# Order of key and value transfers, and the place of the value products, in a cached-attention decode kernel

## The chip, the core and the metric

The kernel runs on one core of a Trainium2 chip. The metric is the device time of one execution in microseconds (us). Engine names follow the profile: PE is TensorE (PEld its weight loads), DVE is VectorE, ACT is ScalarE, POOL is GpSimd, and SP is SyncE, which here only issues DMAs.

## The reference, cut to what matters

One decode step of grouped-query attention over a cache, plus a token-mixing MLP on the same normalised input:

```python
q = (xn @ wq).reshape(B, 1, 32, 128)                  # B = 8 tokens, 32 query heads, 8 key/value heads
scores = einsum("bhqd,bhkd->bhqk", q, k) * 128**-0.5  # cache length 8192, head width 128
p = softmax(scores)
o = einsum("bhqk,bhkd->bhqd", p, v)
y = x + o.reshape(B, 1, 4096) @ wo + mixer(layernorm(xn), w1, b1, w2, b2)
```

All is float32. There are 8 x 8 = 64 pairs of a batch element and a key/value head. The keys of a pair are 8192 x 128 numbers (4096 KB), and so are its values. The query weights `wq` are 8192 KB, the output weights `wo` another 8192 KB.

## The kernel before, in words

**Buffers.** There are two key buffers `K[0]`, `K[1]` and two value buffers `V[0]`, `V[1]`, of 4096 KB each. `wq` is first read into the two value buffers, and `wo` at the end into the two key buffers (`WO`). A pair `s` uses the buffers of index `k = s % 2`. "K63" and "V63" below are the keys and values of pair 63.

**Slots.** The order of the instructions is written out by hand. The function `slot(s, k, ...)` (L365) is called once for each pair: slots 0 and 1 stand ahead of a loop, the loop body holds four slots with a stage boundary between them (L408 to L412), and slots 62 and 63 stand behind it. In a slot:

- DVE turns the keys of the pair in place, four transposes (`turn`, L238), with the transposed probabilities of the pair before between the first and the second (`sm_turn`, L267).
- PE multiplies the probabilities of pair s-1 with its values (`pv`, L274, 16 products), sums the row sums (`o_sums`, L295), adds the mixer's part (`mx_end`, L341), starts the mixer's next part (`mx_begin`, L325), and then makes the scores of pair s (`qk`, L244, 16 products).
- SP issues the values of pair s+1 (L379), which waits until `pv` has left that buffer, and then the keys of pair s+2 (L382), which waits until `qk` has left theirs. In slot 62 the first half of `wo` takes the keys' place, and in slot 63 the second half follows in four pieces (L384, L386).
- DVE picks the result of `pv` (`o_pick`, L279 to L282), PE places it (`o_place`, L285). ACT and POOL do the mixer (`mx_steps`, L329 to L337) beside this.
- Then comes the softmax: the row maximum on DVE (`sm_max`, L250), a small product on PE (L254) with two DVE steps (L255, L256) for the bias, the exponential on ACT (`sm_exp`, L259), the normalising of pair s-1 on DVE (`o_norm`, L298 to L300), and the product that places the probabilities (`sm_place`, L263). The next slot begins with the turning of the next keys.

**The loop's stages.** An engine goes into a slot of the loop only when all engines have finished the slot before the last one. Each engine signals this at a place of its own (`previous_stage_wait`). SP signals it when the transfers issued in that slot have landed.

**The ends.** `prologue_barrier` (L405) stands ahead of slot 0. Ahead of it the queries are projected (L207) and the first keys turned. V0 is issued ahead of the barrier (L358), V1 behind it. After slot 63 the kernel turns the last probabilities, gathers the results of the first seven batch elements (`regroup`, L418 to L423), makes `pv` of pair 63, picks its result (`o_last`, L288 to L291), and multiplies with `wo`: 24 large products (L436), two copies (L439, L440), four folding products (L442) and 32 small products (L445). A copy (L446) and the output DMA (L447) end it.

Of the kernel before, what the change touches and what calls it, by code (L numbers as in the profile page):

```python
# [14 lines left out]
B, D, HQ, HKV, SK, DH, F = 8, 512, 32, 8, 8192, 128, 1792  # L15
REP = HQ // HKV
P = 128
NT = SK // P
Q = 32
NB = P // Q  # L20
NG = NT // 16
NU = NT // NG
BS = Q // B
# [5 lines left out]
N_IT = B * HKV  # L29
NW = 24  # L30
# [4 lines left out]
def attn_mixer_kernel(ctx: ExitStack, tc: tile.TileContext, x, kc, vc, wq, wo, w1, b1, w2, b2, out):  # L35
    nc = tc.nc
# [12 lines left out]
    def misc():  # L49
        turns[0] += 1  # L50
        return MI[turns[0] % 2]
# [5 lines left out]
    V = [ring.tile([P, NT, DH], F32, name=f"v{k}") for k in range(2)]  # L57
# [8 lines left out]
    def load(to, src, n, pieces=(NT,)):  # L66
        rows = src.rearrange("b h (p t) d -> (b h) p t d", p=P)[n]
        at = 0
        for w in pieces:
            nc.sync.dma_start(to[:, at:at + w, :], rows[:, at:at + w, :])  # L70
            at += w
# [4 lines left out]
    def load_wo(a, pieces):  # L76
        rows = wo.rearrange("(p a c) n -> a p c n", p=P, a=2)[a]
        at = 0
        for w in pieces:
            nc.sync.dma_start(WO[a][:, at:at + w, :], rows[:, at:at + w, :])  # L80
            at += w
# [13 lines left out]
    quarter = [slice(j * D // NB, (j + 1) * D // NB) for j in range(NB)]  # L95
# [34 lines left out]
    fold = const.tile([P, Q], F32, name="fold")  # L130
# [19 lines left out]
    OX = const.tile([P, N_IT, REP, NB], F32, name="ox")  # L150
# [14 lines left out]
    xo = const.tile([P, 32, Q], F32, name="xo")  # L165
    nc.vector.memset(xo, 0.0)
    wide = const.tile([P, D], F32, name="wide")
# [4 lines left out]
    O = [ps_o.tile([P, 512], F32, name=f"o{k}") for k in range(2)]  # L172

    MH = ps_h.tile([P, 512], F32, name="mh")
    MI = [ps_m.tile([P, 512], F32, name=f"misc{k}") for k in range(3)]
# [26 lines left out]
    def q_project(between):  # L202
        hw = HKV // 2
        n = REP * DH
        for c in range(NC):
            for h in range(HKV):
                nc.tensor.matmul(S[h // hw][h % hw * Q:(h % hw + 1) * Q, :], xnT[:, c, :], WQ[c][:, h * n:(h + 1) * n],  # L207
                                 start=(c == 0), stop=(c == NC - 1))
        for a in range(2):
            q = t2k.tile([P, n], F32, name="t2k")  # L210
            nc.scalar.copy(q, S[a])
            mt = O[a]
            for r in range(REP):
                nc.tensor.transpose(mt[:, r * P:(r + 1) * P], q[:, r * DH:(r + 1) * DH], ident)
            qs = work.tile([P, hw, REP, B], F32, name="qs")
            nc.scalar.copy(qs, mt.rearrange("p (r h b) -> p h r b", r=REP, b=Q)[:, :, :, :B])
            between(a)
            mq = misc()
            w = hw * REP * B
            for j in range(NB):  # L220
                nc.tensor.matmul(mq[:, j * w:(j + 1) * w], rj[:, j].rearrange("p i d -> p (i d)"),
                                 qs.rearrange("p h r b -> p (h r b)"), start=True, stop=True)
            for h in range(hw):
                nc.vector.tensor_copy(QT[:, :, a * hw + h].rearrange("p b j r -> p j r b"),
                                      mq.rearrange("p (j h x) -> p h j x", j=NB, h=hw)[:, h].rearrange("p j (r b) -> p j r b", r=REP))
        WQ.clear()
# [9 lines left out]
    def turn(k, a, w=NT // 4):  # L236
        t = K[k][:, a:a + w, :].rearrange("p t d -> p (t d)")
        nc.vector.transpose(t, t)  # L238
# [22 lines left out]
    def sm_place(k):  # L261
        m = misc()
        nc.tensor.matmul(m, perm, PR[k], start=True, stop=True)  # L263
        return m
# [6 lines left out]
    def pv(k, u0=0, u1=NU):  # L271
        for u in range(u0, u1):
            c = u % NB
            nc.tensor.matmul(O[k][c * Q:(c + 1) * Q, :], PT[k][:, u * Q:(u + 1) * Q],  # L274
                             V[k][:, u * NG:(u + 1) * NG, :].rearrange("p t d -> p (t d)"),
                             start=(u < NB), stop=(u >= NU - NB))

    def o_pick(k):
        nc.vector.tensor_tensor(OM.rearrange("p (g d) -> p g d", g=NG), O[k].rearrange("p (g d) -> p g d", g=NG),  # L279
                                dm.unsqueeze(2).to_broadcast([P, NG, DH]), ALU.mult)  # L280
        nc.vector.tensor_add(OB, OM[:, :256], OM[:, 256:])
        nc.vector.tensor_add(OB[:, :DH], OB[:, :DH], OB[:, DH:])  # L282

    def o_place(k):
        nc.tensor.matmul(MH[:, k * REP:(k + 1) * REP], OB[:, :DH], sel, start=True, stop=True)  # L285

    def o_last(k):
        nc.vector.tensor_copy(OM[:, :256], O[k][:, :256])  # L288
        nc.scalar.copy(OM[:, 256:], O[k][:, 256:])
        for g in range(NG):  # L290
            nc.tensor.matmul(MH[:, k * REP:(k + 1) * REP], OM[:, g * DH:(g + 1) * DH], selg[:, g, :],  # L291
                             start=(g == 0), stop=(g == NG - 1))

    def o_sums(k):
        nc.tensor.matmul(MH[:, 64 + k * REP:64 + (k + 1) * REP], LR[:, k:k + 1].to_broadcast([P, P]), sel, start=True, stop=True)  # L295

    def o_norm(k, s):
        nc.vector.reciprocal(RD, MH[:, 64 + k * REP:64 + (k + 1) * REP])  # L298
        nc.vector.tensor_tensor(OS, MH[:, k * REP:(k + 1) * REP], RD, ALU.mult)  # L299
        nc.vector.tensor_tensor(OX[:, s], OS.unsqueeze(2).to_broadcast([P, REP, NB]),  # L300
                                block.unsqueeze(1).to_broadcast([P, REP, NB]), ALU.mult)

    proj, mixed = MH[:, P:2 * P], MH[:, 2 * P:3 * P]
# [35 lines left out]
    def mx_end(k):  # L339
        for j in range(NB):  # L340
            nc.tensor.matmul(mixed[j * Q:(j + 1) * Q, :], BW[k], ACC[:, quarter[j]], start=True, stop=True)  # L341
# [5 lines left out]
    m = misc()  # L347
# [7 lines left out]
            turn(0, k * quart)  # L355

    q_project(first_turns)
    load(V[0], vc, 0)  # L358
    q_place(0, 0)
    mx_table()  # L360
    mx_pick(0, 0)

    def slot(s, k, placed, left=2, loop=False):  # L365

        if placed is not None:
            turn(k, 0)
            sm_turn(1 - k, placed)
            for a in range(1, 4):  # L370
                turn(k, a * quart)
            pv(1 - k)
            o_sums(1 - k)
            mx_end(1 - k)
        mx_begin(k)
        if loop:
            tc.previous_stage_wait(nc.tensor.engine)
        if left:
            load(V[1 - k], vc, s + 1)  # L379
        qk(k)  # L380
        if left > 1:
            load(K[k], kc, s + 2)  # L382
        elif left:
            load_wo(0, (NT // REP,))  # L384
        else:
            load_wo(1, (NW - 16, 4, 3, 1))  # L386
        if placed is not None:
            o_pick(1 - k)
            o_place(1 - k)
        mx_steps(k, loop)  # L390
        if left:
            q_place(s + 1, 1 - k)
            mx_pick(1 - k, s + 1)
        if placed is not None:
            y_add()
        if loop:
            tc.previous_stage_wait(nc.vector.engine)
        sm_max(k)
        sm_bias()
        sm_exp(k)  # L400
        if placed is not None:
            o_norm(1 - k, s - 1)
        return sm_place(k)

    tc.prologue_barrier()  # L405
    m = slot(0, 0, None)
    m = slot(1, 1, m)
    with tc.For_i(2, N_IT - 2, 4, iteration_sync="staggered") as s:  # L408
        for n in range(4):
            m = slot(s + n, n % 2, m, loop=True)  # L410
            if n < 3:
                tc.stage_boundary()  # L412
    m = slot(N_IT - 2, 0, m, left=1)
    m = slot(N_IT - 1, 1, m, left=0)

    def regroup(b0, b1, copy):  # L418
        for b in range(b0, b1):
            nc.tensor.matmul(O[0][:, b * Q:(b + 1) * Q], OX[:, b * HKV:(b + 1) * HKV].rearrange("p h r j -> p (h r j)"), fold,  # L420
                             start=True, stop=True)
        copy(xo.rearrange("p c (b s) -> p c b s", s=BS)[:, :, b0:b1, 0],
             O[0][:, b0 * Q:b1 * Q].rearrange("p (b c) -> p c b", c=Q))  # L423

    sm_turn(1, m)
    regroup(0, B - 1, nc.scalar.copy)
    pv(1)
    o_sums(1)
    mx_end(1)
    o_last(1)  # L430
    o_norm(1, N_IT - 1)
    regroup(B - 1, B, nc.vector.tensor_copy)
    y_add()
# [4 lines left out]
        nc.tensor.matmul(proj[j * Q:(j + 1) * Q, :], gather[:, j].rearrange("p b s -> p (b s)"), yacc, start=True, stop=False)  # L438
    nc.vector.tensor_copy(wide[:, :256], S[0][:, :256])  # L439
    nc.scalar.copy(wide[:, 256:], S[0][:, 256:])  # L440
    for j in range(NB):
        nc.tensor.matmul(proj[j * Q:(j + 1) * Q, :], fold, wide[:, quarter[j]], start=False, stop=False)  # L442
    for c in range(NW, 32):
        for j in range(NB):
            nc.tensor.matmul(proj[j * Q:(j + 1) * Q, :], xo[:, c, :], WO[1][:, c - 16, quarter[j]], start=False, stop=(c == 31))  # L445
    nc.vector.tensor_copy(yacc, proj)  # L446
# [29 lines left out]
```

## Time and profile before

| what | value |
|---|---|
| median of 3 runs | 1298.3 us (1298.07 to 1300.26) |
| the profiled execution's own time | 1300.48 us |
| its span in the trace | 1298.7 us |
| bytes read from memory | 553.69 MB, 426 GB/s over the span |
| PE busy, mean granted clock | 905.7 us (70%), 0.77 |
| DVE, ACT, POOL busy | 857.5, 331.3, 218.0 us |

Times in the rows of the trace count from the start of the span. A row of the timeline has the start, the duration, the engine, the line, the operation, its operands with their sizes, and behind an "x" how many instructions it stands for; brackets tell how long the engine was idle before and for what. A row of the windows has the stretch, its length, the busy time of PE, PEld, DVE, ACT and POOL (each with a count), the granted PE clock, the busy share of the DMA engines and their GB/s. A matmul of float32 numbers shows as two records.

### The profile page before, as it was taken

The numbers are of one execution on the slowest core, as the hardware profiler recorded it, in microseconds if no ns is written. First come the engines' busy times: TensorE is split into PE (matmuls) and PEld (weight loads), VectorE is DVE, ScalarE is ACT, GpSimd is POOL, SyncE is SP. The second block draws the span as 40 slices with busy tenths as digits, with TensorE's granted clock in tenths as the row PEclk, the third lists the DMA queues.
The fourth block names the chain that finished last, engine by engine and source line by source line (L and its number), as shares of the span: only waits on it lengthen the run. The fifth ranks groups of instructions, "written<-read, shape, count | busy, mean of one in ns | idle before, by whom it ended". The sixth has DMA issues, their size and how long they took to land.

```text
span 1298.7 us, 15589 instructions
## 1 busy us (share of the span) xinstructions
PE 905.7 (70%) x5498; PEld 271.0 (21%) x5498; DVE 857.5 (66%) x1261; ACT 331.3 (26%) x458; POOL 218.0 (17%) x205
## 2 busy tenths in 40 slices
PE   4657767767767767766766766776766776776777
PEld 1112212212212212212212211221221221211223
DVE  3666766766766776776776776776676676676671
ACT  1223123223223223223223213213213312312321
POOL 1112122122112112112112112112112212212211
PEclk9678778778768778768777777867777877877877
DMA  9999999999999999999999999999999999999994
GB/s 405 435 433 426 432 435 436 436 432 428 432 436 436 435 432 428 433 436 436 434 432 428 434 436 436 434 432 428 434 436 436 433 429 432 434 436 436 433 427 196
DMA packets 19789, 553.84 MB, mean 426 GB/s; under 512 B 2332, under 2 KB 2364, under 8 KB 2628
## 3 DMA queue, kind: packets, MB, share of 16 engines
q1 hardware_dynamic: 19620, 553.67, 98.8%
q8 instruction: 7, 0.11, 0.0%
q0 software_dynamic: 160, 0.04, 0.0%
q14 instruction: 2, 0.02, 0.0%
HBM read 553.69 MB, written 0.02 MB: 426 GB/s over the span
## 4 chain that ended last, share of the span: by engine, by line
PE 58%; DVE 20%; issue 15%; DMA 6%; DVEq 1%; POOL 0%; ACT 0%; POOLq 0%
PE o L274 28%; PE s L244 17%; DVE k L238 8%; PE misc L325 5%; DMA k<-in_A_k_cache_dram 4%; DVE mr L250 3%; DVE pt L267 3%; DMA v<-in_A_v_cache_dram 3%; PE misc L254 2%; PE mh L341 2%; PE mh L285 2%; PE mh L295 2%; DVE sq L255 1%; DVE nb L256 1%; DVE os L299 1%
## 5 line engine op out<-in xcount | busy, mean ns | idle before, releaser
L238 DVE STREAM_TRANSPOSE k<-k 128x2048 f32<-128x2048 f32 x256 | 574.0, 2280 | 154.5 <-issue 131.2
L274 PE MATMUL o<-v,pt 128*32 128x512 f32 x2048 | 370.3, 889 | 193.3 <-DVE pt L267 191.8
L329 ACT ACT_TABLE_LOAD x64 | 82.1, 1283 | 799.0 <-PE misc L325 787.7
L244 PE MATMUL s<-k,w 128*32 128x512 f32 x2048 | 234.6, 599 | 0.0
L332 POOL TENSOR_TENSOR macc<-g,mw 112x512 f32<-112x512 f32 x64 | 66.7, 1042 | 989.4 <-ACT g L329 989.4
L274 PEld LDWEIGHTS o<-v,pt 128*32 128x32 f32 x2048 | 87.0, 155 | 504.4 <-issue 359.2
L263 PE MATMUL misc<-pr,perm 128*128 128x512 f32 x128 | 116.3, 1006 | 105.6 <-ACT pr L259 105.6
L306 DVE TENSOR_TENSOR yacc<-mh,yacc 128x128 f32<-128x128 f32 x64 | 18.7, 292 | 188.2 <-PE mh L285 188.2
L329 ACT ACTIVATE g<-misc,mw 112x512 f32<-112x512 f32 x128 | 99.5, 777 | 79.3 <-POOL macc L332 77.8
L244 PEld LDWEIGHTS s<-k,w 128*32 128x32 f32 x2048 | 60.2, 110 | 166.4 <-issue 140.9
L337 ACT ACT_TABLE_LOAD x64 | 82.1, 1283 | 1.1
L336 POOL TENSOR_TENSOR macc<-macc,g 112x512 f32<-112x512 f32 x64 | 80.8, 1263 | 5.1
L332 POOL TENSOR_TENSOR g<-g,mw 112x512 f32<-112x512 f32 x64 | 66.6, 1040 | 56.9 <-ACT g L329 56.9
L254 PE MATMUL misc<-nident,mr 128*128 128x128 f32 x128 | 31.2, 326 | 62.7 <-DVE mr L250 62.7
L325 PE MATMUL misc<-hn,bm 8*112 8x512 f32 x128 | 71.7, 640 | 0.6 <-DVE mw L315 0.6
L259 ACT ACTIVATE pr<-s,nb 128x512 f32<-128x512 f32 x64 | 44.0, 687 | 35.1 <-DVE rd L298 23.9
L263 PEld LDWEIGHTS misc<-pr,perm 128*128 128x128 f32 x128 | 25.8, 252 | 117.8 <-ACT pr L259 115.9
L250 DVE TENSOR_REDUCE mr<-s 128x1 f32<-128x512 f32 x64 | 43.6, 681 | 6.6 <-PE s L244 6.6
L267 DVE STREAM_TRANSPOSE pt<-misc 128x512 f32<-128x512 f32 x64 | 43.2, 675 | 2.5 <-PE misc L263 2.5
L279 DVE TENSOR_TENSOR om<-o,dm 128x512 f32<-128x512 f32 x63 | 41.7, 662 | 2.5 <-PE o L274 2.1
L255 DVE TENSOR_TENSOR sq<-misc,hmask 128x128 f32<-128x128 f32 x64 | 18.7, 292 | 37.1 <-PE misc L254 37.1
L254 PEld LDWEIGHTS misc<-nident,mr 128*128 128x128 f32 x128 | 19.0, 187 | 69.1 <-DVE mr L250 69.1
(98 smaller groups left out, 378.3 us busy)
## 6 DMA issues: line engine op xcount, KB each, us to landing
v<-in_A_v_cache_dram SPq DMA_DIRECT2D x64, 4096.0 KB, 19.8
k<-in_A_k_cache_dram SPq DMA_DIRECT2D x63, 4096.0 KB, 24.2
v<-in_A_wq_dram SPq DMA_DIRECT2D x2, 4096.0 KB, 17.0
k<-in_A_k_cache_dram SPq DMA_DIRECT2D x2, 2048.0 KB, 30.3
k<-in_A_wo_dram SPq DMA_DIRECT2D x1, 4096.0 KB, 25.2
k<-in_A_wo_dram SPq DMA_DIRECT2D x1, 2048.0 KB, 10.1
k<-in_A_wo_dram SPq DMA_DIRECT2D x1, 1024.0 KB, 12.2
k<-in_A_wo_dram SPq DMA_DIRECT2D x1, 768.0 KB, 13.5
```

Of the source, the lines that this page charges most:

```text
L238: nc.vector.transpose(t, t)
L244: nc.tensor.matmul(S[k][g * Q:(g + 1) * Q, :], W[k][:, j, :], kt[:, g, :, j * Q:(j + 1) * Q], start=(j == 0), stop=(j == NB - 1))
L250: nc.vector.tensor_reduce(MR, S[k], AX.X, ALU.max)
L254: nc.tensor.matmul(m[:, :P], MR.to_broadcast([P, P]), nident, start=True, stop=True)
L263: nc.tensor.matmul(m, perm, PR[k], start=True, stop=True)
L267: nc.vector.transpose(PT[k], m)
L274: nc.tensor.matmul(O[k][c * Q:(c + 1) * Q, :], PT[k][:, u * Q:(u + 1) * Q], V[k][:, u * NG:(u + 1) * NG, :].rearrange("p t d -> p (t d)"), ...
L325: nc.tensor.matmul(MI[2][:FP, :], BM[k].to_broadcast([B, FP]), hn, start=True, stop=True)
L329: nc.scalar.activation(G, MI[2][:FP, :], AF.Gelu_apprx_tanh, bias=MW[k][:, 1, j:j + 1], scale=MW[k][:, 0, j:j + 1])
L332: nc.gpsimd.tensor_tensor(G if j else ACC, G, MW[k][:, 2, j:j + 1].to_broadcast([FP, D]), ALU.mult)
L336: nc.gpsimd.tensor_add(ACC, ACC, G)
L337: nc.scalar.activation(sink, epst[:1], AF.Exp)
```

## The change

Five things change.

1. The values of pair s are issued as the first thing in slot s, no longer in slot s-1. So SP's order becomes: values of pair s, keys of pair s+2. The keys of a pair now stand ahead of the values of the pair before it. V0 is now issued behind the prologue's barrier. In slot 63 the first half of `wo` is issued right behind V63, the second half after `qk` as it was.
2. `pv` of pair s-1 leaves the start of slot s. Its first 8 products stand behind the softmax's bias, its last 8 behind the placing product. PE's stage signal stands between them.
3. `o_pick`, `o_place`, `o_sums` and `o_norm` in slot s are now those of pair s-2.
4. `regroup` of the first seven batch elements goes from behind slot 63 into it, ahead of `qk`, and uses another PSUM buffer.
5. At the end, `pv` of pair 63 stands in two halves around `o_pick` and `o_place` of pair 62, `o_last` stands ahead of `mx_end`, and the four folding products stand behind the first 16 of the 32 small products.

The core of the diff:

```diff
-    load(V[0], vc, 0)
     q_place(0, 0)
...
-    def slot(s, k, placed, left=2, loop=False):
+    def slot(s, k, placed, n, left=2, loop=False):
+        load(V[k], vc, s)
+        if not left:
+            load_wo(0, (NT // REP,))
+        if n:
             turn(k, 0)
             sm_turn(1 - k, placed)
             for a in range(1, 4):
                 turn(k, a * quart)
-            pv(1 - k)
-            o_sums(1 - k)
+        if n > 1:
+            o_sums(k)
+        if n:
             mx_end(1 - k)
         mx_begin(k)
-        if loop:
-            tc.previous_stage_wait(nc.tensor.engine)
-        if left:
-            load(V[1 - k], vc, s + 1)
+        if not left:
+            regroup(0, B - 1, nc.scalar.copy)
         qk(k)
         if left > 1:
             load(K[k], kc, s + 2)
-        elif left:
-            load_wo(0, (NT // REP,))
-        else:
+        elif not left:
             load_wo(1, (NW - 16, 4, 3, 1))
-        if placed is not None:
-            o_pick(1 - k)
-            o_place(1 - k)
+        if n > 1:
+            o_pick(k)
+            o_place(k)
...
         sm_exp(k)
-        if placed is not None:
-            o_norm(1 - k, s - 1)
-        return sm_place(k)
+        if n:
+            pv(1 - k, 0, NU // 2)
+        if loop:
+            tc.previous_stage_wait(nc.tensor.engine)
+        if n > 1:
+            o_norm(k, s - 2)
+        m = sm_place(k)
+        if n:
+            pv(1 - k, NU // 2, NU)
+        return m
...
     sm_turn(1, m)
-    regroup(0, B - 1, nc.scalar.copy)
-    pv(1)
+    pv(1, 0, NU // 2)
+    o_pick(0)
+    o_place(0)
+    o_sums(0)
+    o_norm(0, N_IT - 2)
+    pv(1, NU // 2, NU)
     o_sums(1)
+    o_last(1)
     mx_end(1)
-    o_last(1)
     o_norm(1, N_IT - 1)
...
-    for j in range(NB):
-        nc.tensor.matmul(proj[j * Q:(j + 1) * Q, :], fold, wide[:, quarter[j]], start=False, stop=False)
     for c in range(NW, 32):
+        if c == NW + 4:
+            for j in range(NB):
+                nc.tensor.matmul(proj[j * Q:(j + 1) * Q, :], fold, wide[:, quarter[j]], start=False, stop=False)
```

**SP, start of the program.** The rows show what SP issues before the loop, with the semaphores that it waits for. Here `k_81`, `k_82` are the two key buffers and `v_83`, `v_84` the two value buffers. Before:

```order
L70 DMA k_81<-in_A_k_cache_dram 128x4096 x2
L70 DMA k_82<-in_A_k_cache_dram 128x8192
L70 DMA v_83<-in_A_v_cache_dram 128x8192 [waits DMAHW0_49,PE_49]
L70 DMA v_84<-in_A_v_cache_dram 128x8192 [waits barrier_Pool_Activation_PE_DVE_SP_release,DMAHW1_49,PE_49]
L70 DMA k_81<-in_A_k_cache_dram 128x8192 [waits DMAHW2_49,DMAHW3_49,DVE_49,PE_49]
```

V0 (the first row of `v_83`) waited only for the transfer of `wq` and the PE products that read it. The same stretch of the changed kernel:

```order
L70 DMA k_81<-in_A_k_cache_dram 128x4096 x2
L70 DMA k_82<-in_A_k_cache_dram 128x8192
L70 DMA v_83<-in_A_v_cache_dram 128x8192 [waits barrier_Pool_Activation_PE_DVE_SP_release,DMAHW0_49,PE_49]
L70 DMA k_81<-in_A_k_cache_dram 128x8192 [waits DMAHW2_49,DMAHW3_49,DVE_49,PE_49]
L70 DMA v_84<-in_A_v_cache_dram 128x8192 [waits DMAHW1_49]
```

V0 now waits for the barrier, and K2 (the second row of `k_81`) stands ahead of V1.

**SP, end of the program.** The rows are the last transfers of the loop, the loop's end, and what follows. Before, the values of `v_83` are V62, the keys K63, and `v_84` behind the loop is V63:

```order
L70 DMA v_83<-in_A_v_cache_dram 128x8192
L70 ISA
L70 DMA k_82<-in_A_k_cache_dram 128x8192
L408 REGISTER_ALU
L408 COMPARE_AND_BRANCH
L408 UNCONDITIONAL_BRANCH
L70 DMA v_84<-in_A_v_cache_dram 128x8192
L80 DMA k_81<-in_A_wo_dram 128x8192
```

In the changed kernel K63 is the last transfer of the loop, ahead of V62 and V63:

```order
L70 DMA k_82<-in_A_k_cache_dram 128x8192
L421 REGISTER_ALU
L421 COMPARE_AND_BRANCH
L421 UNCONDITIONAL_BRANCH
L70 DMA v_83<-in_A_v_cache_dram 128x8192
L70 DMA v_84<-in_A_v_cache_dram 128x8192
L80 DMA k_81<-in_A_wo_dram 128x8192
```

K63 moved by one transfer of 4096 KB towards the start, and V62 by one towards the end. V63 and `wo` kept their places.

**PE, one slot of the loop.** Here `s_176` takes the scores, `o_178` and `o_177` the value products, `misc_180` and `misc_181` the small products of the softmax. Before:

```order
L274 MATMUL o_177<-v_83,pt_153 32x512 x16
L295 MATMUL mh<-sel,lr 128x4
L341 MATMUL mh<-macc,bw_171 32x128 x4
L325 MATMUL misc_182<-hn,bm_170 112x512
L244 MATMUL s_176<-k_82,w_152 32x512 x16
L285 MATMUL mh<-sel,ob 128x4
L254 MATMUL misc_180<-nident,mr 128x128
L263 MATMUL misc_181<-pr_156,perm 128x512
```

And in the changed kernel:

```order
L295 MATMUL mh<-sel,lr 128x4
L341 MATMUL mh<-macc,bw_171 32x128 x4
L325 MATMUL misc_182<-hn,bm_170 112x512
L244 MATMUL s_176<-k_82,w_152 32x512 x16
L285 MATMUL mh<-sel,ob 128x4
L254 MATMUL misc_180<-nident,mr 128x128
L274 MATMUL o_177<-v_83,pt_153 32x512 x8
L263 MATMUL misc_181<-pr_156,perm 128x512
L274 MATMUL o_177<-v_83,pt_153 32x512 x8
```

The value products moved from the time in which DVE turns the keys to both sides of the placing product.

More of the change, by code (lines that the diff above doesn't have):

```diff
@@ L393, in slot @@
             mx_pick(1 - k, s + 1)
-        if placed is not None:
+        if n:
             y_add()
@@ L400, in slot, with regroup @@
         sm_exp(k)
-        if placed is not None:
-            o_norm(1 - k, s - 1)
-        return sm_place(k)
+        if n:
[5 more added lines that the diff above has]
+        m = sm_place(k)
+        if n:
+            pv(1 - k, NU // 2, NU)
+        return m
+    def regroup(b0, b1, copy):
+        for b in range(b0, b1):
+            nc.tensor.matmul(MI[0][:, b * Q:(b + 1) * Q], OX[:, b * HKV:(b + 1) * HKV].rearrange("p h r j -> p (h r j)"), fold,
+                             start=True, stop=True)
+        copy(xo.rearrange("p c (b s) -> p c b s", s=BS)[:, :, b0:b1, 0],
+             MI[0][:, b0 * Q:b1 * Q].rearrange("p (b c) -> p c b", c=Q))
     tc.prologue_barrier()
-    m = slot(0, 0, None)
-    m = slot(1, 1, m)
+    m = slot(0, 0, None, 0)
+    m = slot(1, 1, m, 1)
     with tc.For_i(2, N_IT - 2, 4, iteration_sync="staggered") as s:
         for n in range(4):
-            m = slot(s + n, n % 2, m, loop=True)
+            m = slot(s + n, n % 2, m, 2, loop=True)
             if n < 3:
                 tc.stage_boundary()
[L413 to L423, printed above, removed]
-    sm_turn(1, m)
-    regroup(0, B - 1, nc.scalar.copy)
-    pv(1)
+    m = slot(N_IT - 2, 0, m, 2, left=1)
+    m = slot(N_IT - 1, 1, m, 2, left=0)
+    sm_turn(1, m)
+    pv(1, 0, NU // 2)
[4 more added lines that the diff above has]
+    pv(1, NU // 2, NU)
     o_sums(1)
+    o_last(1)
     mx_end(1)
-    o_last(1)
     o_norm(1, N_IT - 1)
```

## The prediction

> **What bounds the kernel now.** I read the page's slices and queues first, since a kernel that moves 554 MB may be bound by its transfers.
>
> ```profile
> DMA  9999999999999999999999999999999999999994
> GB/s 405 435 433 426 432 435 436 436 432 428 432 436 436 435 432 428 433 436 436 434 432 428 434 436 436 434 432 428 434 436 436 433 429 432 434 436 436 433 427 196
> q1 hardware_dynamic: 19620, 553.67, 98.8%
> ```
>
> The DMA engines are busy in every slice but the last. The windows place the end of that, and the rows of DVE give the pace of the loop: each slot starts when its keys land.
>
> ```profile
> 40.00:1270.00 1230.00, 868.91 (x5202) 254.56 (x5202) 834.47 (x1201) 325.72 (x446) 213.47 (x192) 0.76 1.00 433
> 1270.00:1281.00 11.00, 9.94 (x40) 4.92 (x44) 1.29 (x5) 1.35 (x3) 0.61 (x1) 0.55 0.94 400
> 1281.00:1283.30 2.30, 2.30 (x27) 1.15 (x19) 0.42 (x1) 0.37 (x1) 0.00 (x0) 0.93 0.24 95
> 1283.30:1298.70 15.40, 10.52 (x135) 4.72 (x135) 1.63 (x7) 0.37 (x1) 0.00 (x0) 0.88 0.01 2
> ...
> 72.53 2.31 DVE L238 STREAM_TRANSPOSE k<-k 128x2048 f32<-128x2048 f32 x1 [4.25 <-DMA k<-in_A_k_cache_dram]
> 1253.72 2.31 DVE L238 STREAM_TRANSPOSE k<-k 128x2048 f32<-128x2048 f32 x1 [2.94 <-DMA k<-in_A_k_cache_dram]
> ```
>
> From K2 (72.53) to K63 (1253.72) are 61 slots of 19.36 us. Two transfers of 4.194 MB at 433 GB/s are 19.37 us. So the loop runs at the pace of the DMA, which has no gap, and one transfer of 4096 KB takes 9.68 us. The transfers end near 1281.6 (0.24 x 2.3 us into the third window). The last 17 us of the span move nothing. The chain that ended last and SP's issues show what fills them.
>
> ```profile
> 1229.71 23.92 DMA k<-in_A_k_cache_dram
> ...
> 1275.96 6.24 PE o L274 x32
> 1282.20 0.32 PE mh L295 x2
> ...
> 1285.39 6.75 PE s L436 x48
> ...
> 1295.26 0.29 DVE yacc L446
> ```
>
> K63 lands at 1253.63, and turning, scores, softmax, the value product of pair 63, `wo` and the output follow one another. V63 and all of `wo` land meanwhile, so the last value product, which ends at 1282.20, is late by computation and not by data.
>
> **The change, part by part.** *Bytes.* The same transfers are made. If the DMA still has no gap, it ends where it did, plus what the start loses.
>
> *The start.* V0 now waits for the barrier. Its price is a possible gap behind K1.
>
> ```profile
> 0.75 0.86 SPq L63 DMA_DIRECT2D v<-in_A_wq_dram  x2
> 40.49 0.33 SPq L70 DMA_DIRECT2D v<-in_A_v_cache_dram  x1
> 47.73 0.33 SPq L70 DMA_DIRECT2D k<-in_A_k_cache_dram  x1
> 49.62 2.30 DVE L238 STREAM_TRANSPOSE k<-k 128x2048 f32<-128x2048 f32 x1
> ...
> 0.00:2.00 2.00, 0.00 (x0) 0.00 (x0) 0.00 (x0) 1.24 (x1) 0.93 (x6) 1.00 0.53 147
> 0.00:20.00 20.00, 6.37 (x36) 1.81 (x36) 7.89 (x33) 1.87 (x3) 3.92 (x13) 1.00 0.95 395
> 20.00:40.00 20.00, 7.63 (x64) 3.88 (x64) 11.75 (x16) 1.61 (x4) 0.00 (x0) 0.80 0.98 419
> ```
>
> By 40 us, 7.90 + 8.38 = 16.28 MB have moved. `wq`, K0 and K1 are 16.78 MB, so K1 runs until 41.15. V1 left right behind the barrier at 40.49, and V0 will now leave there. At the start of the run 0.29 MB had moved by 2.00, which is 0.68 us of full rate, so data flowed 0.6 us after the issue at 0.75. That would put V0's data at 41.1: no gap. The upper bound is the output transfer, issued at 1295.58 (row below), whose whole way takes until the span's end, 3.1 us: a gap of 2.4. I take 0.5 us, nearer to the first row. K2 is issued after the first scores (47.73) while V0 runs until 51, so nothing starves behind it.
>
> *The loop.* Rows of two slots give the pieces:
>
> ```profile
> 1225.93 3.64 PE L244 MATMUL s<-k,w 128*32 128x512 f32 x32
> 1230.87 0.49 PE L254 MATMUL misc<-nident,mr 128*128 128x128 f32 x2 [0.98 <-DVE mr L250]
> 1232.47 0.18 DVE L300 TENSOR_TENSOR ox<-os,block 128x16 f32 x1
> 1233.01 1.59 PE L263 MATMUL misc<-pr,perm 128*128 128x512 f32 x2 [1.66 <-ACT pr L259]
> 1234.47 2.31 DVE L238 STREAM_TRANSPOSE k<-k 128x2048 f32<-128x2048 f32 x1 [1.82 <-issue]
> 1237.30 6.66 DVE L238 STREAM_TRANSPOSE k<-k 128x2048 f32<-128x2048 f32 x3
> ...
> 1244.14 3.64 PE L244 MATMUL s<-k,w 128*32 128x512 f32 x32
> ```
>
> Scores start 9.7 us after the first turn (1244.14 - 1234.47), and DVE's last step of the softmax ends 3.1 us after the scores (1232.65 - 1229.57). So the next turn can start after 12.8 + q us, where q is the time of `qk`. Before, `qk` followed the value product directly and ran at full clock in 3.64 us. Now PE has little to do while DVE turns the keys, and `qk` comes behind a pause. What that costs is told by rows that come behind a pause:
>
> ```profile
> 42.43 5.24 PE L244 MATMUL s<-k,w 128*32 128x512 f32 x32
> 53.33 6.61 PE L274 MATMUL o<-v,pt 128*32 128x512 f32 x32 [1.57 <-DMA v<-in_A_v_cache_dram]
> 42.00:43.00 1.00, 1.00 (x5) 0.20 (x8) 0.00 (x0) 0.47 (x1) 0.00 (x0) 0.50 1.14 492
> 46.00:48.00 2.00, 1.66 (x16) 0.24 (x8) 0.18 (x1) 0.75 (x2) 1.64 (x2) 1.00 1.21 524
> L274 PE MATMUL o<-v,pt 128*32 128x512 f32 x2048 | 370.3, 889 | 193.3 <-DVE pt L267 191.8
> ```
>
> The first `qk` began at a clock of 0.50 and took 5.24; wholly at half clock it would be 7.3. I take 5.3, the row of the same product behind a pause, and a slot needs 18.1 us (16.4 to 20.1). The transfers give it 19.36, so the cover is 1.2 us and the edit costs nothing; beyond it every 0.1 us would cost 6 us over 62 slots. The Trainium skill, "TensorE: Matmul & The Clock Gate", section "Part 1: The HAM clock gate", says that PE runs at half rate after an idle window of about 3.4 us, and at full rate only after a busy window of that length. By that page `qk` would turn fast 3.4 to 6.8 us after its start, an estimate of 5.3 to 7.0 us for q and 18.1 to 19.8 for a slot; the trace agrees as to the half clock behind the pause.
>
> The softmax's own chain fits too: 1.3 us from scores to L254, 0.5 for it, half a value product (1.8 at full clock, as half of 3.64; 3.3 as half of 6.61), the placing product (1.6), then the other half. With q = 5.3 the value buffer is free 22 to 26 us after its slot's start. Values issued then have to start 38.7 us after it (four transfers later), and keys, issued after 15 us, 29.0 us after it. Each queue has over 12 us in hand. SP's signal, which waits for the transfers of the slot before the last, names keys that the slot needs anyway.
>
> *The end.* K63 now goes ahead of V62, so it lands at 1253.63 - 9.68 + 0.5 = 1244.4. V63 and `wo` keep their places:
>
> ```profile
> 1242.57 0.34 SPq L70 DMA_DIRECT2D v<-in_A_v_cache_dram  x1
> 1267.70 2.22 SPq L80 DMA_DIRECT2D k<-in_A_wo_dram  x4
> 1295.58 0.70 SPq L447 DMA_DIRECT2D out_dram<-yacc  x1
> ...
> L80 SPq DMA_DIRECT2D k<-in_A_wo_dram x5: 328/368/901, 1247.8 to 1269.0; - x5
> ...
> k<-in_A_wo_dram SPq DMA_DIRECT2D x1, 256.0 KB, 13.7
> ```
>
> The last piece of `wo` lands at 1269.0 + 13.7 = 1282.7, with the start's loss 1283.2. Behind it stand only the last small products and the copy; before, the copy began 3.44 us ahead of the span's end (1298.7 - 1295.26). With 0.3 us for the products this floor is 1283.2 + 0.3 + 3.4 = 1286.9 us.
>
> The engines may be later. From 1244.4: scores begin 9.7 us on and end at 1259.4 (q = 5.3), L254 ends 1.8 us on at 1261.2; then four halves of value products and the placing product in a row. At full clock these are 4 x 1.8 + 1.1 = 8.3 us, ending at 1269.5. At the mean of the group (370.3 / 64 = 5.8 for a whole product) they are 4 x 2.9 + 1.6 = 13.2 us, ending at 1274.4. From that end to the copy it was 13.1 us (1282.20 to 1295.26); the folding products behind half of the small ones hide some 0.4 of that in the wait for the copies, so 12.7. `regroup` in slot 63 lies under the turning and costs nothing; its 2.8 us also leave the chain of the end. At full clock the engines reach the copy at 1282.2, ahead of the floor; at the mean clock at 1287.1, and the span is 1290.5. PE has no pause behind `qk` here, so I lean to the faster case: 1288.6 us, 10.1 less than 1298.7.
>
> **The sum.** Span 1298.7 - 10.1 = 1288.6. The profiled execution's own time was 1300.48 and the median of the runs 1298.3; taking the 10.1 off the median gives 1288.2.
>
> **The rivals.** *A: the engines become the bound.* PE's pause makes `qk` slow in each slot, and the next turn waits for the softmax behind it. Slot 1 turns at 49.62, so slot 63 starts at 49.6 + 62c for a slot of c us. At c = 19.27 that is 1244.4, and nothing is lost; at 19.45 the whole gain is gone; at 19.7 it is 1271.0, 26.6 us late, and the time is 1315. For it: the half clock in rows above, and q = 6.9 is enough. Against it: `qk` itself is work that brings the clock back within 4 us (42.43 to 46). By that page of the Trainium skill c would be 18.9 in the mean, an estimate below the deciding 19.45. Chance of a loss beyond 0.2%: 0.08; of c near 19.45 and no change: 0.03.
>
> *B: the DMA gets gaps.* V63 waits for the second half of the value product of pair 61, 22 to 26 us into slot 62, and V62, ahead of it on the queue, is through 29.0 us into it. With a slow clock and slow issue it may be late by up to 2 us, and V0 by 2.4. Everything behind shifts: a span of 1290.5 to 1292.5, so 1290 to 1292. Against it stand the slacks worked out above. Chance 0.12, still faster.
>
> *C: the start of slot 63 is not the bound.* If the end is held by `wo` alone with no loss at the start, the floor is 1286.4, and the time 1286.0. Inside my forecast's range.
>
> **The chances.** The forecast (a loop at the DMA's pace, an end shortened by 8 to 12 us) has 0.77, B 0.12, A 0.11. The range goes from C (1286.0) to the end at the mean clock together with B's gap (1290.5 - 1298.7 + 1298.3 = 1290.1, plus 2.4) = 1292.5. About 0.2%, 2.6 us, is what a measurement of this kernel can tell: the three runs lie 2.2 us apart. Faster by more than that 0.89, within it 0.03, slower 0.08.
>
> **What would show it.** Right: the windows still show a share of 1.00 and 433 GB/s from 40 to 1270, slots of 19.36 us that start at the landing of keys, K63's first turn near 1244, and 6 to 8 us between the last transfer and the span's end. The row of `qk` should stand at 5 to 6 us in place of 3.64. Wrong: DVE's first turn waiting for its own softmax and not for keys (A), a gap in the DMA near 41 or near 1253 (B), or a last `wo` product that starts after 1281.

## The result and the profile after

The changed kernel takes 1289.8 us (median of 4 runs, 1289.41 to 1290.11), the kernel before 1298.35 us beside it (4 runs, 1298.07 to 1300.26). The ratio is 0.9931 (95% interval 0.9914 to 0.9948): 8.55 us less, where 10.1 were forecast. A later set of runs, nine of the kernel before and five of the changed one beside them, gave 1300.24 and 1289.6 us: 10.6 us less. The experiment "Before, again" says why the kernel before gives two such medians. The profiled execution of the changed kernel took 1290.11 us, its span is 1288.2 us.

First the slices' GB/s and the queue on the page after:

```profile
GB/s 408 418 428 437 427 435 439 426 438 432 431 439 426 436 434 430 438 427 435 436 428 438 431 432 439 425 438 433 430 439 427 435 436 428 438 429 433 439 426 348
q1 hardware_dynamic: 19620, 553.67, 99.7%
```

The last slice moves 348 GB/s where it moved 196, and the queue's share rose from 98.8% to 99.7%. The bytes are the same, so the time saved is time in which nothing was moved. The windows after (us from the span's start, length, then busy time of PE, PEld, DVE, ACT and POOL, the granted clock, the DMA's share and GB/s) say where:

```profile
42.00:43.00 1.00, 1.00 (x5) 0.20 (x8) 0.00 (x0) 0.31 (x2) 0.00 (x0) 0.50 0.13 33
40.00:1260.00 1220.00, 830.92 (x5176) 241.76 (x5176) 871.20 (x1191) 326.31 (x447) 216.12 (x192) 0.80 1.00 433
1260.00:1272.00 12.00, 10.70 (x84) 3.48 (x76) 4.96 (x15) 0.80 (x3) 0.00 (x0) 1.00 0.98 421
1282.00:1283.30 1.30, 1.16 (x40) 0.89 (x35) 0.00 (x0) 0.25 (x1) 0.00 (x0) 1.00 0.43 167
```

The loop keeps a share of 1.00 at 433 GB/s. The microsecond from 42 to 43 moves 33 GB/s, where before it moved 492: that is the gap of the start, 0.9 us. Counted at the full rate, the transfers then end near 1282.5 (0.43 x 1.3 us into the fourth window), 5.7 us before the span's end; before, counted the same way, they ended near 1281.6, 17.1 us ahead of it. That is 11.4 us less behind the data and 0.9 us more ahead of its end: 10.5 us of span, 1298.7 to 1288.2.

The chain that ended last, after (start, duration, what), then the record of SP's last four issues of `wo` (shortest, median and longest, first and last start) and the time from issue to landing of the last two:

```profile
1221.04 23.93 DMA k<-in_A_k_cache_dram
...
1245.06 2.31 DVE k L238
...
1261.66 21.98 DMA k<-in_A_wo_dram
...
1283.68 1.12 PE mh L456 x32
...
1284.82 0.29 DVE yacc L457
...
L80 SPq DMA_DIRECT2D k<-in_A_wo_dram x4: 328/427/432, 1260.8 to 1262.1; - x4
k<-in_A_wo_dram SPq DMA_DIRECT2D x1, 768.0 KB, 22.0
k<-in_A_wo_dram SPq DMA_DIRECT2D x1, 256.0 KB, 22.1
```

K63 is turned at 1245.06 and no longer at 1253.72. The chain before ran from K63 to the copy over the engines, 48 records of `wo` products (6.75 us) among them; now it runs through a transfer of `wo`, with 16 small products (32 records) and the copy behind it. With its 21.98 us that transfer is the piece of 768 KB, the last but one, which lands at 1283.64. The last piece, of 256 KB, lands near 1284.2 (1262.1 + 22.1). Only the last 4 of the 16 products need it; 12 of 16 take some 0.8 of the 1.1 us, so PE comes to them near 1284.5 and does not wait. PE's rows of the end say how near the engines are to that floor:

```profile
1279.42 1.92 PE L446 MATMUL s<-k,xo 128*32 128x512 f32 x16 [0.94 <-DMA k<-in_A_wo_dram]
...
1283.68 1.08 PE L456 MATMUL mh<-k,xo 128*32 128x128 f32 x32 [0.52 <-DMA k<-in_A_wo_dram]
```

PE waits for `wo` at the last large products for 0.94 us: the engines are ahead of the data, but by no more than that.

The loop pays elsewhere for what it got. These are the scores and the value products, first in the page before, then in the page after (busy us and mean ns of one):

```profile
L244 PE MATMUL s<-k,w 128*32 128x512 f32 x2048 | 234.6, 599 | 0.0
```

```profile
L244 PE MATMUL s<-k,w 128*32 128x512 f32 x2048 | 372.6, 894 | 324.6 <-DVE k L238 324.6
L274 PE MATMUL o<-v,pt 128*32 128x512 f32 x2048 | 246.0, 598 | 0.0
```

The half clock behind PE's pause has moved from the value products (370.3 before, 246.0 after) to the scores: 372.6 / 64 = 5.82 us for a pair. The waits of DVE ahead of its turns (us in all, times, longest), and its first turn in slot 1, give what is left of the cover:

```profile
DVE k L238 <- issue: 45.7, 50, 1.7
...
50.81 2.30 DVE L238 STREAM_TRANSPOSE k<-k 128x2048 f32<-128x2048 f32 x1
```

From 50.81 to 1245.06 are 62 slots of 19.26 us. DVE waits ahead of its first turn for 45.7 us in all, 0.74 us a slot; before, the same wait was 131.2 us. The 19.26 and the 0.74 are means over two stretches. From 89.64 to 276.97 are ten slots of 18.73 us in the mean, in which DVE waits only twice (1.2 us in all): the keys are there, and the engines set the pace. That shows the engines' slot directly, 18.6 us without the two waits. The rows at both ends of that stretch:

```profile
89.64 2.31 DVE L238 STREAM_TRANSPOSE k<-k 128x2048 f32<-128x2048 f32 x1
...
276.97 2.31 DVE L238 STREAM_TRANSPOSE k<-k 128x2048 f32<-128x2048 f32 x1
```

From 276.97 to 1245.06 the slots are 19.36 us, the transfers' pace of before, and DVE waits 0.88 us a slot. There the transfers set the slot, with little to spare.

### The profile page after: what moved, and what is told of

Its sections match the earlier page's. It is cut to its first block, busy times and chain, and to the rows that moved or that the text cites. A ratio compares the mean times of both kernels' runs of the same rounds, so it can differ in the third digit from the quotient of the medians.

```text
span 1288.2 us, 15580 instructions
## 1 busy us (share of the span) xinstructions
PE 866.7 (67%) x5498; PEld 256.0 (20%) x5498; DVE 897.4 (70%) x1261; ACT 331.3 (26%) x458; POOL 220.0 (17%) x205
## 3 DMA queue, kind: packets, MB, share of 16 engines
q1 hardware_dynamic: 19620, 553.67, 99.7%
## 4 chain that ended last, share of the span: by engine, by line
DVE 49%; PE 35%; issue 9%; DMA 6%; DVEq 0%; SPq 0%; ACT 0%; ACTq 0%
DVE k L238 39%; PE s L244 28%; DMA k<-in_A_k_cache_dram 4%; DVE pt L267 3%; DVE mr L250 2%; PE misc L254 2%; DMA k<-in_A_wo_dram 2%; PE mh L285 2%; DVE sq L255 1%; PE o L274 1%; DVE nb L256 1%; DVE os L299 1%; PE misc L263 1%; DVE ox L300 1%; DVE rd L298 1%
## 5 line engine op out<-in xcount | busy, mean ns | idle before, releaser
L238 DVE STREAM_TRANSPOSE k<-k 128x2048 f32<-128x2048 f32 x256 | 574.0, 2280 | 61.7 <-issue 45.7
L244 PE MATMUL s<-k,w 128*32 128x512 f32 x2048 | 372.6, 894 | 324.6 <-DVE k L238 324.6
L274 PE MATMUL o<-v,pt 128*32 128x512 f32 x2048 | 246.0, 598 | 0.0
L244 PEld LDWEIGHTS s<-k,w 128*32 128x32 f32 x2048 | 87.0, 156 | 603.0 <-issue 408.3
L306 DVE TENSOR_TENSOR yacc<-mh,yacc 128x128 f32<-128x128 f32 x64 | 18.6, 291 | 230.7 <-PE mh L285 230.7
L329 ACT ACT_TABLE_LOAD x64 | 82.1, 1283 | 315.7 <-PE misc L325 306.1
L336 POOL TENSOR_TENSOR macc<-macc,g 112x512 f32<-112x512 f32 x64 | 83.1, 1298 | 5.1
L337 ACT ACT_TABLE_LOAD x64 | 82.1, 1283 | 1.2
L274 PEld LDWEIGHTS o<-v,pt 128*32 128x32 f32 x2048 | 53.5, 109 | 132.6 <-issue 125.0
L263 PE MATMUL misc<-pr,perm 128*128 128x512 f32 x128 | 73.0, 652 | 1.6 <-ACT pr L259 1.6
L281 DVE TENSOR_TENSOR ob<-om 128x256 f32<-128x256 f32 x63 | 50.1, 795 | 2.2
L282 DVE TENSOR_TENSOR ob<-ob 128x128 f32<-128x128 f32 x63 | 37.2, 591 | 2.2
## 6 DMA issues: line engine op xcount, KB each, us to landing
k<-in_A_wo_dram SPq DMA_DIRECT2D x1, 2048.0 KB, 18.6
```

The costliest lines, as they stand in the source:

```text
L244: nc.tensor.matmul(S[k][g * Q:(g + 1) * Q, :], W[k][:, j, :], kt[:, g, :, j * Q:(j + 1) * Q], start=(j == 0), stop=(j == NB - 1))
L329: nc.scalar.activation(G, MI[2][:FP, :], AF.Gelu_apprx_tanh, bias=MW[k][:, 1, j:j + 1], scale=MW[k][:, 0, j:j + 1])
L336: nc.gpsimd.tensor_add(ACC, ACC, G)
L337: nc.scalar.activation(sink, epst[:1], AF.Exp)
```

## The experiments

The theory that all runs test is that of the prediction: the loop is at the DMA's pace, the engines need about 18 to 18.6 us of a slot's 19.36, and the gain is the earlier K63 at the end. The rivals are an engine-bound loop (A) and gaps in the transfers (B). Edits are shown against the changed kernel where nothing else is said.

**Transfers' order alone.** The changed order of transfers (values of pair s first in slot s, then keys of pair s+2) on the engines' order of before: `pv` whole ahead of `qk`, the end as before. The main lines of the edit, against the kernel before:

```diff
-    load(V[0], vc, 0)
...
+        load(V[k], vc, s)
+        if not left:
+            load_wo(0, (NT // REP,))
...
-        if left:
-            load(V[1 - k], vc, s + 1)
         qk(k)
```

> The kernel before with the order of transfers alone changed: values of a pair issued first thing in its slot, behind the keys of the next pair; value products whole and ahead of the scores, as before. Theory (the order helps only if the scores do not stand behind the value product on PE): the value product waits for values that land 9.7 us after the keys, the loop still runs at 19.36 us a slot with each slot some 7 us behind its keys, and the end is as long as before: 1296 to 1298.5, little or no gain. Rival (the order is what counts): 1289 to 1291.

Measured: 1296.64 us (10 runs, 1296.1 to 1299.4), ratio to before 0.9986 (0.9976 to 0.9995), 1298.25 us beside it. PE's waits and pieces of the chain that ended last:

```profile
PE o L274 <- DMA v<-in_A_v_cache_dram: 182.2, 60, 3.7
...
1208.01 27.24 DMA v<-in_A_v_cache_dram
...
1252.51 2.30 DVE k L238
```

In 60 slots the value product waits for its values, 3.0 us each. The keys land early, but the scores stand behind that product on PE, and K63 is turned at 1252.51, only 1.2 us earlier than before. So the order of the transfers alone is worth 1.6 us: early keys are used only if the scores go ahead of the values' work.

**Engines' order alone.** The new order of the instructions with the old order of transfers: values of pair s+1 and keys of pair s+2 issued at the end of slot s.

```diff
+    load(V[0], vc, 0)
...
     def slot(s, k, placed, n, left=2, loop=False):
-        load(V[k], vc, s)
...
+        if left:
+            load(V[1 - k], vc, s + 1)
+        if left > 1:
+            load(K[k], kc, s + 2)
```

> The changed kernel's order on the engines with the old order of transfers: values of pair s+1 ahead of keys of pair s+2, both issued at the end of slot s, since the value buffer is free only there. Theory (the two halves need each other): the queue runs dry in each slot, a slot takes about 21 us, two transfers plus the wait for the buffer, and the time is 1385 to 1405. Rival (the order on the engines brings the gain by itself): 1289 to 1298.

Measured: 1569.09 us (one run), far beyond both figures. The window from 100 to 1500, and the rows of one slot, SP's and DVE's:

```profile
100.00:1500.00 1400.00, 817.83 (x4804) 230.16 (x4808) 774.66 (x1119) 299.50 (x412) 197.62 (x177) 0.71 0.84 352
...
620.95 2.31 DVE L238 STREAM_TRANSPOSE k<-k 128x2048 f32<-128x2048 f32 x1 [4.79 <-issue]
...
643.56 0.33 SPq L70 DMA_DIRECT2D v<-in_A_v_cache_dram  x1
644.13 0.33 SPq L70 DMA_DIRECT2D k<-in_A_k_cache_dram  x1
644.91 2.31 DVE L238 STREAM_TRANSPOSE k<-k 128x2048 f32<-128x2048 f32 x1 [4.96 <-issue]
```

A slot is 23.96 us (644.91 - 620.95), the DMA's share 0.84. The queue does run dry, as expected, but that is not the whole of it. SP can issue the values only when the second half of the value product has left their buffer, at 643.56; DVE's next turn starts 0.45 us behind the end of SP's issues. Nothing that the trace names holds DVE there ("issue"), but the keys that it turns were issued at 620.31, and two transfers of keys in this stretch took 21.1 us to land (median), so they were there near 641.4. So I take it that the slot's boundary holds all engines until SP is through its own slot, with SP blocked behind the value product; this was not tried by itself. What the run shows is that the new order of the engines needs transfers that are not issued behind its last product. It does not show that half of the change is worth nothing in every other arrangement.

**The value product whole, ahead of the placing product.**

```diff
         if n:
-            pv(1 - k, 0, NU // 2)
+            pv(1 - k)
...
         m = sm_place(k)
-        if n:
-            pv(1 - k, NU // 2, NU)
```

> The changed kernel with the value product in one piece ahead of the placing product, in place of halves around it. Theory (the cycle from one turning of the probabilities to the next bounds a slot next to DVE's own): 0.7 (turning) + 6.7 (three turns of keys) + 5.8 (scores) + 1.3 + 0.5 (softmax to the bias) + 3.7 (whole value product at full clock) + 1.1 (placing) + 0.1 = 19.9 us a slot, 0.5 to 0.6 above the transfers' 19.3, so slot 63 starts some 20 to 40 us later: 1310 to 1330. Rival (the halves make no difference, DVE's chain alone counts): 1289.5 to 1291.

Measured: 1334.43 us (one run), 4 us above the upper figure. One cycle of the chain that ended last:

```profile
631.01 0.04 DVE pt L267
...
631.65 6.67 DVE k L238 x3
...
638.45 6.20 PE s L244 x32
...
646.45 3.57 PE o L274 x32
...
651.11 0.72 DVE pt L267
```

The cycle is 20.1 us (651.11 - 631.01), and no DMA stands in it: the last three turns, the scores, the softmax, the whole value product and the placing product, whose result DVE needs between the first turn and the second. The engines set the slot. The halves are what keeps 1.8 us of value product out of this cycle.

**How much cover a slot has.** Transposes whose result is read by nothing, on DVE at the end of each slot of the loop: one of 128x256 in the first kernel (0.44 us by its own record), two of 128x512 in the second.

```diff
+        if loop:
+            nc.vector.transpose(OM[:, :256], OM[:, :256])
```

```diff
+        if loop:
+            nc.vector.transpose(OM[:, :512], OM[:, :512])
+            nc.vector.transpose(OM[:, :512], OM[:, :512])
```

> The changed kernel with one DVE transpose of 128x256 on scratch added at the end of each slot of the loop, some 0.35 us on the chain that bounds a slot from the engines' side. DVE waited some 0.75 us a slot for keys in the changed kernel, so its slot is 18.6 us against 19.36 of the transfers. Theory: still covered, within 1 us of the changed kernel. Rival (no cover left): 62 x 0.35 = 22 us slower.

> As the run with one small transpose, but with two of 128x512, 1.35 us a slot. Theory: the slot becomes 18.6 + 1.35 = 19.95 us, 0.6 to 0.7 us above the transfers', and slot 63 starts some 35 to 45 us later: 1325 to 1335. Rival (the cover is larger than DVE's waits show): 1290 to 1292.

Measured: 1289.74 us with the small one, and 1333.89 us with the two large ones (one run each). DVE's rows in the second, first the turn in slot 1, then the two added steps of one slot, then the turn of K63, its waits ahead of the first turns, and the group of the scores:

```profile
49.65 2.30 DVE L238 STREAM_TRANSPOSE k<-k 128x2048 f32<-128x2048 f32 x1
...
609.08 0.70 DVE L407 STREAM_TRANSPOSE om<-om 128x512 f32<-128x512 f32 x1
609.82 0.71 DVE L408 STREAM_TRANSPOSE om<-om 128x512 f32<-128x512 f32 x1
...
1291.52 2.30 DVE L238 STREAM_TRANSPOSE k<-k 128x2048 f32<-128x2048 f32 x1
...
DVE k L238 <- issue: 0.4, 1, 0.4
L244 PE MATMUL s<-k,w 128*32 128x512 f32 x2048 | 392.9, 937 | 351.5 <-DVE k L238 351.5
```

The slot is (1291.52 - 49.65) / 62 = 20.03 us in the mean; the loop's 60 slots have the added steps. DVE hardly waits any more (0.4 us in all), so this is the engines' own slot. The scores take longer here, 392.9 / 64 = 6.14 us, so the prediction's formula, 12.8 + q, gives 12.8 + 6.14 + 1.41 = 20.35 us with the added steps, 0.3 too much. For the changed kernel it gives 12.8 + 5.82 = 18.6 us, beside the 18.6 of its first stretch. So the formula holds to some 0.3 us. The cover in the waits is 0.74 us in the mean and 0.88 where the transfers set the pace. One small step fits into it: DVE's waits fell from 45.7 to 31.8 us in all, and the time stayed. The 1.41 us do not fit and cost 44 us.

**Is it the clock that takes the cover?** Three products whose result is read by nothing fill PE's pause ahead of the scores in each slot of the loop.

```diff
+        if loop:
+            for _ in range(3):
+                nc.tensor.matmul(O[1 - k], ident, rj.rearrange("p j i d -> p (j i d)"), start=True, stop=True)
```

> The changed kernel with three products of 128x128 by 128x512 added ahead of the scores in the loop, whose results nobody reads, so that PE has no pause while DVE turns the keys. Theory (the slow clock of the scores lies under the transfers): the scores take 3.6 to 4 us in place of 5.8, DVE waits some 2 us a slot longer for keys, and the time stays within 0.5 us of the changed kernel. Rival (the engines hold the loop back here and there): 2 us or more faster.

Measured: 1289.72 us (6 runs, 1289.46 to 1291.54). The group of the scores on the page, and DVE's waits:

```profile
L244 PE MATMUL s<-k,w 128*32 128x512 f32 x2048 | 304.3, 748 | 228.4 <-DVE k L238 228.4
...
DVE k L238 <- issue: 114.7, 59, 3.2
```

The mean granted clock is 0.93 in place of 0.81, the scores take 4.75 us a pair in place of 5.82 (not the 3.6 to 4 that I expected), and DVE's wait grows by 69 us, 1.1 us a slot and not the 2 expected. The time does not move: in this loop PE's clock buys cover and nothing else. Then both additions in one kernel, the three products and the two large transposes:

> PE filled in its pause and two DVE transposes of 1.35 us added in each slot. With the pause filled DVE waited 1.1 us a slot longer for keys than in the changed kernel (130 us in place of 61), so the slot should be 18.6 - 1.1 + 1.35 = 18.85 us. Theory (the clock of the scores takes the cover away): covered, 1289 to 1291.5. Rival (the added DVE work itself is what costs, whatever PE does): 1325 to 1335 as with the transposes alone.

Measured: 1289.56 us (one run). DVE's waits here:

```profile
DVE k L238 <- issue: 38.0, 39, 1.9
```

The 44 us are gone. With q = 4.72 (302.3 us for the 64 pairs) the formula gives 12.8 + 4.7 + 1.4 = 18.9 us, under 19.36. So rival A's mechanism is there, and what decides whether it strikes is the clock of the scores.

**The end.** The old end on the new loop: `regroup` behind slot 63, `pv` of pair 63 whole, `o_last` and the folding products where they stood.

```diff
-        if not left:
-            regroup(0, B - 1, nc.scalar.copy)
...
+    regroup(0, B - 1, nc.scalar.copy)
...
-    pv(1, NU // 2, NU)
+    pv(1)
...
-        if c == NW + 4:
```

> The changed kernel's loop and order of transfers with the end as it was before: regroup of seven batch elements behind slot 63, the value product of pair 63 in one piece, mx_end ahead of o_last, the folding products ahead of all small products. Theory (the gain comes from the keys' place in the queue; the edits of the end only keep the engines ahead of the last pieces of wo, by 0.9 us): 1 to 2.5 us slower than the changed kernel, 1291 to 1292.5. Rival (the edits of the end bring most of the gain): 1294 to 1298.

Measured: 1291.42 us (5 runs, 1290.35 to 1291.76). Of its chain of the end:

```profile
1276.27 7.10 PE s L444 x48
...
1286.48 0.29 DVE yacc L454
```

The end is on the engines again, and the copy starts 1.7 us later (1286.48 against 1284.82). So the edits of the end are worth 1.6 us in the medians (1291.42 - 1289.8), until they meet the floor of `wo`. Its five executions lie in two groups, though, two near 1290.4 and three from 1291.4 to 1291.8, so in a single execution the edits are worth some 0.6 to 2 us. The rest of the gain, some 7 us in the medians, is the order.

**The start.** V0 issued ahead of the barrier again, all else as in the changed kernel. The second set of runs has the changed kernel beside it on the same chip, since a microsecond was in question.

```diff
+    load(V[0], vc, 0)
...
-        load(V[k], vc, s)
+        if n:
+            load(V[k], vc, s)
```

> The changed kernel with V0 issued at its old place, ahead of the prologue's barrier. Theory (the loop and the end are paced by the transfers, and the start's gap of some 0.9 us near 42 us in the trace of the changed kernel shifts everything behind it): the gap is gone and the time is 0.7 to 1.2 us lower than the changed kernel's 1289.8, so 1288.6 to 1289.1. Rival (the engines' chain sets the end): no change, 1289.5 to 1290.1.

> The changed kernel with V0 issued ahead of the prologue's barrier, as in the first run of this, now beside the changed kernel on one chip. Theory (the start's gap is passed on whole): 0.8 to 1.3 us below the changed kernel. Rival (the difference of the first run came from the chip): within 0.4 us of it.

> The changed kernel itself, beside the same kernel with V0 issued early on the same chip. Theory: 1289.4 to 1290.1 in most executions, as before.

Measured: 1288.75 us (6 runs, 1288.6 to 1290.83), then 1289.17 us (5 runs, 1288.70 to 1289.92) beside 1289.6 us (5 runs, 1289.38 to 1290.03) of the changed kernel. The window of the gap and the last of the chain, in the profile of the first set:

```profile
42.00:43.00 1.00, 1.00 (x6) 0.20 (x8) 0.00 (x0) 0.31 (x2) 0.00 (x0) 0.50 1.14 492
...
1283.41 0.29 DVE yacc L459
```

The gap is gone, and the copy starts 1.4 us earlier in the profile. The medians differ by 0.4 to 1.1 us, but two of the six executions of the first set, at 1290.61 and 1290.83, lie above every one of the changed kernel's. In the second set both kernels have a ratio of 0.9919 to before (intervals to 0.9904 and 0.9905 below, 0.9933 above). The gap and its direction are shown; that it costs a full microsecond of time is not. This is the only version here that may beat the changed kernel, and by no more than can be settled.

**Before, again.** The question was why before's profiled execution lay 2.2 us above its median.

> The kernel before, unchanged, for a second profile. The profiled execution of before had a span of 1298.7 us and a time of 1300.48, 2.2 us above the median, while the changed kernel's executions lie within 0.7 us. Theory (before, the end is a chain of engines and depends on where PE's clock stands when it begins; after, the end is paced by transfers): a span of about 1296.5 with shorter products behind the last scores (value product, regroup and placing product 2 us less in all). Rival (the loop's transfers differ): the first turn of K63 lies about 2 us earlier and the end has the same length of 45.0 us.

Measured: 1301.73 us (one run), a span of 1300.0, the other way from what I had hoped to see. Its chain at the end, and a window of the `wo` products in the first profile and in this one:

```profile
1253.77 2.31 DVE k L238
...
1285.12 8.30 PE s L436 x48
...
1296.54 0.29 DVE yacc L446
...
1288.00:1291.00 3.00, 3.00 (x32) 0.87 (x28) 0.00 (x0) 0.00 (x0) 0.00 (x0) 0.98 0.00 0
1288.00:1291.00 3.00, 3.00 (x16) 0.58 (x12) 0.00 (x0) 0.00 (x0) 0.00 (x0) 0.50 0.00 0
```

The turn of K63 stands where it stood (1253.72 in the first profile), and so does the start of the `wo` products (1285.39). The 48 records take 8.30 us in place of 6.75; less the 0.27 us by which they start earlier, that is 1.28, the whole difference of the two spans (1300.0 and 1298.7). The window shows where: from 1285 to 1288 the granted clock is 0.50 in both profiles; from 1288 to 1291 it is 0.98 in the first, where PE makes 32 records, and still 0.50 in the second, where it makes 16. In the kernel with the transfers' order alone the clock is 1.00 from 1283 to 1289, and the same 48 records take 5.40 us. So an end on the engines depends on where PE's half clock falls.

Over three sets of runs 33 executions of before lie in three groups: 18 from 1297.6 to 1298.3, 7 from 1300.1 to 1300.6, 8 from 1301.1 to 1301.8. A median of a few executions therefore depends on how many fall into each group: it was 1298.25 us in one of these sets and 1300.24 in another. The two profiles are of the second and third group. The first group would fit an end like that of the transfers-alone kernel: `wo` products of 5.40 us in place of 6.75 and a last value product of 5.35 in place of 6.24 are 2.2 us less. But no execution of that group was profiled, so this is not shown. The changed kernel's nine executions lie from 1289.38 to 1290.11; its end waits for a transfer.

## Why the prediction was right, point by point

- **The loop at the DMA's pace, no gap:** right, share 1.00 and 433 GB/s. Rival B's gap in the loop did not appear. The slots of 19.36 us that start at the landing of keys are right from 276.97 on; in the ten slots up to there, the engines set the pace at 18.73 us with the keys already there, which the working did not foresee and which costs nothing.
- **The start, 0.5 us (0 to 2.4):** 0.9 us in the trace. The nearer bound was the right one to lean to, though the 0.5 was too low.
- **The scores, q = 5.3 us (3.64 to 7.3):** 5.82 in the mean; single ones take 5.0 to 6.6. A slot needs some 18.6 us and not 18.1, and the cover is 0.74 to 0.88 us, not 1.2. The row of the first `qk` was one of 64, in which the clock rose from 0.50 early; in the mean of all it rises later.
- **The limit of rival A:** the mechanism is real. The kernel stands 0.7 to 0.9 us a slot from a loss. With slots of 20.03 us, 0.77 above its own 19.26, it lost 44 us, about 60 times the excess, as the prediction's 6 us for 0.1 us has it.
- **K63 at 1244.4:** its turn stands at 1245.06, the landing at 1244.97. Of the 0.6 us between the landings, 0.4 is the start's larger gap.
- **The end:** PE was at a clock of 1.00 from 1260 to 1283, the case that the prediction leaned to. The engines reach `wo` ahead of it, and the floor decides. But the floor was put 1.3 us too low, at 1286.9 where the span is 1288.2. It was added up along the last piece of `wo`: landing at 1283.2, then 0.3 us of products, then 3.4. That piece lands near 1284.2. What the products wait for last is the piece ahead of it, which lands at 1283.64 with 1.1 us of products behind it. The 3.4 us behind the copy's start are as forecast. Of the 1.0 us by which the last piece is late against the forecast, 0.4 is the start's larger gap; the rest is not traced. The likeliest span, 1288.6, stood between the two cases worked out, 1286.9 and 1290.5. That it lies 0.4 us from the measured one is in part luck, since the case that came had a floor priced too low.
- **`regroup` under the turning, folding products under the copies' wait:** right; the chain goes through neither.
- **The sum:** the span fell by 10.5 us, forecast 10.1. The step that failed is the last one, "taking the 10.1 off the median". Before's profiled execution lay 2.2 us above its median (1300.48 against 1298.3), and after's lies at its own (1290.11 against 1289.8). By the second profile of before, an end on the engines differs from execution to execution with the clock, so a part of those 10.1 us probably belonged to that one execution. Taken as own time against own time, 1300.48 - 10.1 = 1290.4 is 0.3 us from the profiled 1290.11. The median moved by 8.55 here and by 10.6 in the later set: before's median lay in another group there, while the changed kernel's was 1289.8 and then 1289.6.

## What to carry to other kernels

Where a loop runs at the pace of its transfers, an order that brings the last-needed data earlier pays at the end only if the engines' order uses it at once: each half of this change alone gave 1.6 us or lost 271. What such a reorder takes in return is each slot's cover, so work out the engines' slot against the transfers' with the clock that a new pause brings, and test it by adding a known amount of work. Compare a span with the span of the other kernel and not with a median, above all where an end on the engines varies with the clock; and look at single executions for groups before a difference of medians is read to a microsecond.

## What the runs showed of the hardware

DVE's small additions of the result (L281, 128x256, both inputs in SBUF) took longer where they now lie beside POOL's addition of the mixer. The rows of that line in before, in after, and of two such places after (durations as min/median/max in ns):

```profile
L281 DVE TENSOR_TENSOR ob<-om x63: 424/426/427, 60.8 to 1263.8; 128x256 f32<-128x256 f32 x63
```

```profile
L281 DVE TENSOR_TENSOR ob<-om x63: 424/598/1506, 80.8 to 1268.1; 128x256 f32<-128x256 f32 x63
...
1216.26 1.27 POOL L336 TENSOR_TENSOR macc<-macc,g 112x512 f32<-112x512 f32 x1
...
1216.42 1.40 DVE L281 TENSOR_TENSOR ob<-om 128x256 f32<-128x256 f32 x1
...
1042.12 0.43 DVE L281 TENSOR_TENSOR ob<-om 128x256 f32<-128x256 f32 x1
1042.15 1.52 POOL L336 TENSOR_TENSOR macc<-macc,g 112x512 f32<-112x512 f32 x1
```

The same addition takes 1.40 us when POOL's started 0.16 us ahead of it; where it starts 0.03 us ahead of POOL's it takes 0.43, and POOL's takes 1.52 in place of 1.27. Over the 63 places the time goes with the lead: wherever POOL's (L336) starts 0.04 to 1.09 us ahead, its lead and DVE's duration add up to 1.54 to 1.56 us. The Trainium skill, "SBUF — State Buffer", section "Who interferes with whom", says that a DVE instruction with two inputs in SBUF contends with a GpSimd instruction that reads SBUF, and the trace agrees: 424 to 427 ns before, where all 63 are alike, and up to 1506 after. It costs nothing here, since DVE then waits for the scores anyway (L306 sits 230.7 us idle for them, in 62 waits).
